# Row-maxima instructions on VectorE: own 8-bit pieces for the throw-away output in place of one shared bf16 tile

## The chip, the cores and the metric

The kernel runs on one core of a Trainium2 chip. The metric is the device time of one execution in microseconds. The kernel before took 447.98 us in the median of three runs (447.98 to 450.43). The profiled execution is one more run of the same program, with its own span.

## What is computed

An attention layer with a cumulative bias feeds a soft mixture of experts. Cut to what matters here:

```python
def _attn_ref(q, k, v, s):            # 8 batches, 8 heads, 576 positions, head size 64
    scores = scale * np.matmul(q, k.transpose(0, 1, 3, 2))
    cum = np.cumsum(np.maximum(s, 0.0), axis=-1)
    bias = -(cum[:, :, :, None] - cum[:, :, None, :])
    scores = np.where(causal, -1000000000.0, scores + np.minimum(bias, 0.0))
    scores = scores - np.max(scores, axis=-1, keepdims=True)
    attn = np.exp(scores)
    attn = attn / (np.sum(attn, axis=-1, keepdims=True) + 1e-09)
    return np.matmul(attn, v)
```

The result, as 4608 rows of 512, goes through a soft routing to 8 experts with 4 slots each (two softmaxes of x @ phi, one over rows and one over slots), two matrix products per expert, and a product back to 4608 x 512 outputs. The part of interest is `np.max(scores, axis=-1)`, the maximum of each row of scores.

## The kernel before, in words

**Stages.** The first stage, up to about 352 us, is attention. Its unit is a pair p of heads (32 pairs, four to a batch, the two heads on partitions 0 to 63 and 64 to 127 of the operands). Weights of the experts are fetched beside it as far as there is room. Then follow the end of the last batch, the experts (L960, L994) and the product back to the outputs (L1026 to L1030).

**One pair.** ScalarE splits the loaded q and k into a rounded part (L282, `cast`) and VectorE into the rest (L287, `low`). TensorE makes the scores once in a rough form for the maxima alone (L315, `mxp`, tile `mx`): queries on partitions, keys along the columns, in four groups i, each into two PSUM banks, one for each head a. VectorE takes the row maxima from these banks (L327, `red`). POOL splits the maxima into two parts (L342, L343, `f0`, tile `mh`), TensorE turns them (L350), ScalarE copies them, and a small DMA lays them into a tile `g` beside the cumulative sums (L363, `md`). Then TensorE makes the exact scores, transposed and with maxima and bias already subtracted (L381, `sc`, tile `s`), ScalarE exponentiates (L392), POOL cuts the causal triangle (L399) and adds up columns for the row sums (L425 to L431), TensorE multiplies with v (L482, tile `y`) and adds up the sums (L511, tile `sum`).

**Once a batch.** VectorE inverts the sums (L599, L600), they make a round trip through HBM (L604, then L521, tile `rs`), VectorE scales each pair's result (L544, `nr`), TensorE transposes it (L552) and works out the logits (L623, L627), and the routing's softmaxes follow (L668 to L783).

**PSUM.** The tiles `mx`, `s` and some others share six banks. A group of `mx` or of `s` takes two. A bank of `mx` is free again when VectorE has read it, a bank of `s` when ScalarE has.

**The row maxima.** One call of `red` handles one group for one head. A pair has 12 such instructions: two of 288 columns with the mask (group 0, chunk 4 of the queries), two each of 320 and 192 columns (group 3), two each of 448 and 64 columns (group 2; the one of 64 columns lies on partitions 64 to 127), and two of 288 columns that start from group 0's maxima (group 1, the scalar `m[:, a, 4:5]`). Each adds the mask to the scores, takes the maximum along the columns and writes that to a column of the tile `mx0`, `mx1` or `mx2` in SBUF. On the chip it is two instructions: the main one (`CUSTOM_DVE_ANT_0`), which also writes every sum of score and mask to a tile called `junk` that nobody reads, and a short one (`DVE_READ_ACCUMULATOR2_ANT`) that writes out the maximum. `junk` is one bf16 tile of 128 x 448 with a single buffer, so each main instruction writes over what the one ahead of it wrote.

**Order.** Every engine runs its instructions in the order that the function `schedule` sets at build time from a table of priorities (`PR`) and estimated durations. The framework then adds semaphore waits where two instructions touch the same bytes and at least one writes. An engine's own semaphore counts its finished instructions; VectorE's is called `DVE_49`. An instruction carries one wait; a second one stands ahead of it as an `EVENT_SEMAPHORE` of its own.

Of the kernel before, what the change touches and what calls it, by code (L numbers as in the profile page):

```python
# [11 lines left out]
BF16 = mybir.dt.bfloat16  # L12
# [90 lines left out]
def tile_attn_softmoe(ctx: ExitStack, tc, qk, v, s, phi, w1, w2, cst, out):  # L103
# [42 lines left out]
    ar, o = {}, 0  # L146
# [16 lines left out]
    one = actx.enter_context(tc.tile_pool(name="one", bufs=1))  # L163
    p2 = actx.enter_context(tc.tile_pool(name="p2", bufs=2))
# [37 lines left out]
    cumd = pd.tile([NH, 2, S], F32, tag="cum", name="cumd", bufs=1)  # L202

    ph = one.tile([128, HP, NS], F32, name="ph")


    mask = one.tile([128, S], F32, name="mask")
# [42 lines left out]
    def own(kind, i, n):  # L250
        live[kind, i % n] = i
# [4 lines left out]
    def scores(p):  # L256
# [4 lines left out]
        gt, w = gs[p % NG], ws[p % NW]  # L261
# [56 lines left out]
        def red(i, a):  # L318
            if i == 0 and a == 0:
                own("mx", p, 3)  # L320
            ps = st["m", p, i][a]
            for (d, c, lo, hi) in groups[i]:
                r = slice(64, 128) if c == 0 else slice(0, 128)
                w = hi - lo
                o = 576 - sum(QC[c]) + lo
                junk = p2.tile([128, 448], BF16, tag="junk", name="junk", bufs=1)
                nc.vector.tensor_tensor_reduce(  # L327
                    out=junk[r, 0:w], in0=ps[r, d:d + w], in1=mask[r, o:o + w], scale=1.0,
                    scalar=m[:, a, 4:5] if i == 1 else NEG, op0=ALU.add, op1=ALU.max, accum_out=m[r, a, c:c + 1])
        mxt = (265, 265, 560, 490)  # L330
        rdt = (480, 540, 900, 760)
        for i in range(4):
            op(("mx", p, i), "PE", mxt[i], (tu, ("mx", i)), (mxp, i),
               [("cast", p, 0), ("cast", p, 1), ("cum", p), dep("f0", old(3))], bank=2, mode=1)
            for a in range(2):
                op(("red", p, i, a), "DVE", rdt[i], (tu + 0.1 * a, ("red", i)), (red, i, a),
                   [("mx", p, i), ("red", p, 0, a) if i else None], frees=[(("mx", p, i), a)])
# [539 lines left out]
    for i in range(o // F):  # L877
        d = []
# [63 lines left out]
    def bk(name):  # L942
        return ps4.tile([128, 512], F32, tag="bk", name=name)

    ps = bk("sit")
# [173 lines left out]
```

## Time and profile before

| | |
|---|---|
| median of three runs | 447.98 us (447.98 to 450.43) |
| profiled execution, from first to last instruction | 447.8 us |
| granted TensorE clock, mean | 0.980 |
| TensorE busy | 414.7 us, 93% |
| VectorE busy | 317.0 us, 71% |
| POOL busy | 279.7 us, 62% |
| ScalarE busy | 250.8 us, 56% |
| main instructions of the row maxima | 384 (320 without and 64 with the scalar) |

In the rows below a line begins with the place in the code, the engine and the operation, then the tile written and the tiles read. PE is TensorE, DVE is VectorE, ACT is ScalarE, SP is the queue that issues DMAs. A busy TensorE is not TensorE at its peak, since the ends of matmuls are modelled and a slow sequence reads as busy too. The chain is the one that ended last, followed back from the last instruction to whatever released it.

### The profile page before, as it was taken

Reading aid. Unit: us, or ns where it says so; the run is one execution under the profiler, and the core shown is the slowest. Engines: PE = TensorE matmul, PEld = TensorE weight load, DVE = VectorE, ACT = ScalarE, POOL = GpSimd, SP = SyncE. Lnnn points to the kernel's source line nnn. Section 1 sums busy time; section 2 is a strip of 40 time slices with the busy share of each in tenths; the row PEclk is TensorE's granted clock in tenths of the full one; section 3 lists DMA queues with packets and bytes.
Section 4 is the critical chain, followed back from the end, with each engine's and each line's share of the span. In section 5 each row is a group of like instructions: output and inputs, shape, how many; then the busy total and the mean of one; then the engine's idle time right before and its main releaser. Section 6 shows DMA issues by size and latency. Waiting matters only on the chain.

```text
span 447.8 us, 14714 instructions
## 1 busy us (share of the span) xinstructions
PE 414.7 (93%) x5637; PEld 310.4 (69%) x5637; DVE 317.0 (71%) x1038; ACT 250.8 (56%) x732; POOL 279.7 (62%) x384
## 2 busy tenths in 40 slices
PE   8889999899999998999899989999999998898960
PEld 8767777687677777877677767778777776434550
DVE  7787778767888787688887887788878575221460
ACT  3146776476558664867486648666755765121350
POOL 8049888758796986588769876987888720000000
PEclk9999999899999998999999999999999999999995
DMA  5416456545554565356455643363337489999988
GB/s 173 146 46 202 152 156 206 139 127 166 167 161 145 177 186 144 113 178 186 124 146 180 182 133 101 118 162 92 103 88 200 132 271 356 344 389 410 347 276 293
DMA packets 54549, 83.01 MB, mean 185 GB/s; under 512 B 5456, under 2 KB 41936, under 8 KB 54480
## 3 DMA queue, kind: packets, MB, share of 16 engines
q1 hardware_dynamic: 54480, 82.09, 58.4%
q8 instruction: 44, 0.72, 0.7%
q14 instruction: 25, 0.20, 0.2%
HBM read 71.64 MB, written 10.06 MB: 182 GB/s over the span
## 4 chain that ended last, share of the span: by engine, by line
PE 67%; DVE 13%; DMA 5%; issue 5%; POOL 4%; ACT 2%; SPq 1%; DVEq 0%; POOLq 0%
PE s L381 20%; PE y L482 13%; DVE junk L327 9%; PE mx L315 9%; PE sum L511 4%; PE m L994 3%; PE m L960 3%; DMA arena<-rs 3%; PE busy L920 3%; DMA rs<-sr 2%; PE nat L552 2%; PE po L1026 2%; DVE arena L544 2%; PE lt L623 1%; PE mt L350 1%
## 5 line engine op out<-in xcount | busy, mean ns | idle before, releaser
L327 DVE CUSTOM_DVE_ANT_0 junk<-mx,mask 128x448 bf16<-128x448 f32 (+2 forms) x320 | 138.0, 431 | 48.5 <-PE mx L315 18.9
L392 ACT ACTIVATE arena<-s 128x288 f32<-128x288 f32 (+4 forms) x384 | 119.0, 397 | 39.0 <-PE s L381 37.9
L381 PE MATMUL s<-w 64*128 64x288 f32 (+4 forms) x1152 | 116.6, 308 | 7.0 <-DVE mx L327 6.4
L381 PEld LDWEIGHTS s<-w 64*128 64x128 f32 (+1 forms) x1152 | 88.4, 179 | 18.4 <-DVE mx L327 6.2
L482 PE MATMUL y<-arena 128*64 128x512 f32 (+4 forms) x640 | 93.1, 428 | 1.3 <-ACT arena L494 0.9
L399 POOL TENSOR_SCALAR_AFFINE_SELECT arena<-arena 128x256 f32<-128x256 f32 (+1 forms) x160 | 69.5, 452 | 22.7 <-ACT arena L392 22.3
L482 PEld LDWEIGHTS y<-arena 128*64 128x64 f32 x640 | 41.1, 136 | 46.5 <-issue 31.4
L425 POOL TENSOR_TENSOR arena<-arena 128x896 f32<-128x896 f32 x31 | 68.1, 2197 | 2.8 <-PE sum L511 0.5
L381 PE MATMUL s<-g 64*128 64x288 f32 (+4 forms) x384 | 66.3, 294 | 0.0
L315 PE MATMUL mx<-w 64*128 64x288 f32 (+4 forms) x384 | 61.1, 304 | 2.3 <-DVE acc L783 1.1
L315 PE MATMUL mx<-g,ones 64*128 64x288 f32 (+4 forms) x384 | 56.9, 302 | 0.0
L287 DVE TENSOR_TENSOR w<-arena,w 128x576 fp32r<-128x576 f32 x64 | 49.9, 813 | 1.4 <-ACT w L282 1.4
L342 POOL TENSOR_SCALAR mh<-mx 128x10 fp32r<-128x10 f32 x32 | 20.9, 654 | 46.3 <-DVE mx L327 46.2
L427 POOL TENSOR_TENSOR arena<-arena 128x640 f32<-128x640 f32 x31 | 48.0, 1550 | 2.6
L282 ACT CAST w<-arena 128x576 fp32r<-128x576 f32 x64 | 39.8, 678 | 12.1 <-DMA arena<-in_qk_dram 12.1
L315 PEld LDWEIGHTS mx<-w 64*128 64x128 f32 x384 | 41.7, 187 | 4.8 <-DVE mx L327 1.7
L381 PEld LDWEIGHTS s<-g 64*128 64x128 f32 (+1 forms) x384 | 44.3, 180 | 0.1
L315 PEld LDWEIGHTS mx<-g,ones 64*128 64x128 f32 x384 | 41.4, 187 | 0.6
L327 DVE CUSTOM_DVE_ANT_0 junk<-mx,mask,mx 128x288 bf16<-128x288 f32 x64 | 33.2, 518 | 9.3
L544 DVE TENSOR_TENSOR arena<-arena 128x576 f32<-128x576 f32 x31 | 31.1, 1031 | 3.9 <-DMA arena<-rs 3.8
L429 POOL TENSOR_TENSOR arena<-arena 128x384 f32<-128x384 f32 x31 | 31.5, 1015 | 2.4
L559 ACT COPY arena<-nat 128x512 f32<-128x512 f32 x32 | 17.5, 588 | 25.8 <-PE nat L552 24.8
(158 smaller groups left out, 548.7 us busy)
## 6 DMA issues: line engine op xcount, KB each, us to landing
pre<-in_w_dram SPq DMA_DIRECT2D x38, 512.0 KB
arena<-in_qk_dram SPq DMA_DIRECT2D x32, 576.0 KB
arena<-in_w_dram SPq DMA_DIRECT2D x19, 512.0 KB
arena<-rs SPq DMA_DIRECT2D x62, 144.0 KB
arena<-in_v_dram SPq DMA_DIRECT2D x32, 256.0 KB
out_dram<-arena SPq DMA_DIRECT2D x11, 512.0 KB
out_dram<-pre SPq DMA_DIRECT2D x6, 512.0 KB
wg<-in_w_dram SPq DMA_DIRECT2D x5, 512.0 KB
```

The costliest lines, as they stand in the source:

```text
L282: nc.scalar.copy(w[:, QO + S * i:QO + S * (i + 1)], st["raw", p][:, i, :])
L287: nc.vector.tensor_tensor(w[:, QO + S * (2 + i):QO + S * (3 + i)], st["raw", p][:, i, :], w[:, QO + S * i:QO + S * (i + 1)].bitcast(F32), ...
L315: nc.tensor.matmul(ps[a][:, d:d + hi - lo], l[r], t[r, KO + lo:KO + hi], start=t is w, stop=t is gt)
L327: nc.vector.tensor_tensor_reduce(out=junk[r, 0:w], in0=ps[r, d:d + w], in1=mask[r, o:o + w], scale=1.0, scalar=m[:, a, 4:5] if i == 1 else ...
L381: nc.tensor.matmul(ps[a][0:n, d:d + hi - lo], t[r, ko + 128 * j:ko + 128 * j + n], t[r, qo + lo:qo + hi], start=x == 0, stop=x == 3)
L392: nc.scalar.activation(st["p", p][0:n, a, o + lo:o + hi], ps[0:n, d:d + hi - lo], AF.Exp, bias=0.0, scale=0.125)
L399: nc.gpsimd.affine_select(d, d, pattern=[[0, 2], [1, n]], compare_op=ALU.is_ge, fill=0.0, base=0, channel_multiplier=-1)
L425: eng.tensor_tensor(z[:, :, 128:576], pt[:, :, 128:576], pt[:, :, 576:1024], op=ALU.add)
L427: eng.tensor_tensor(z[:, :, 256:576], z[:, :, 256:576], pt[:, :, 1024:1344], op=ALU.add)
L429: eng.tensor_tensor(z[:, :, 384:576], z[:, :, 384:576], pt[:, :, 1344:1536], op=ALU.add)
L482: nc.tensor.matmul(y[r, lo - 64:512], vt[:, j, r], st["p", p][:, g, OFF[j] + lo - 128 * j:OFF[j] + 576 - 128 * j], start=(j == 0), stop=(j ...
L544: nc.vector.tensor_tensor(u, u, st.pop(("r", p)), op=ALU.mult)
```

## The change

The shared tile `junk` goes. One tile of 128 x 2 x 1600 bytes is made at the start in the pool `one`, and each main instruction writes into its own piece of it, as 8-bit unsigned numbers: one half for each head a, and in it 64, 192, 320 and 448 bytes for the chunks c = 0, 1, 2, 3 and twice 288 bytes for chunk 4 (groups 1 and 0).

```diff
     ph = one.tile([128, HP, NS], F32, name="ph")
+    junk = one.tile([128, 2, 1600], mybir.dt.uint8, name="junk")
...
                 o = 576 - sum(QC[c]) + lo
-                junk = p2.tile([128, 448], BF16, tag="junk", name="junk", bufs=1)
+                k = [0, 64, 256, 576, 1024][c] + (288 if i == 0 else 0)
                 nc.vector.tensor_tensor_reduce(
-                    out=junk[r, 0:w], in0=ps[r, d:d + w], in1=mask[r, o:o + w], scale=1.0,
+                    out=junk[r, a, k:k + w], in0=ps[r, d:d + w], in1=mask[r, o:o + w], scale=1.0,
                     scalar=m[:, a, 4:5] if i == 1 else NEG, op0=ALU.add, op1=ALU.max, accum_out=m[r, a, c:c + 1])
```

The number and order of instructions on every engine stay as they were; a line is added, so that L327 becomes L328. What changes is waits. In the two places below, `ISA junk` is a main instruction and `ISA mx_108` or `mx_110` a short one (the rows left out are short ones alike).

On VectorE, group 3 of pair 10 stood thus before (it opens the run that begins at 202.21 us in the trace; the last row is the `low` that follows that run, which waits for ScalarE and for a DMA, but not for VectorE):

```order
L327 ISA junk,mx_108<-mx_10_0_2053,mask 128x320 [waits PE_49]
L327 ISA mx_108 128x1
L327 ISA junk,mx_108<-mx_10_0_2053,mask 128x192 [waits DVE_49]
...
L327 ISA junk,mx_108<-mx_10_1_2054,mask 128x320 [waits DVE_49,PE_49]
...
L327 ISA junk,mx_108<-mx_10_1_2054,mask 128x192 [waits DVE_49]
...
L287 TENSOR_TENSOR w_134<-arena,w_134 128x576 [waits DMAHW5_49,Activation_49]
```

and stands thus with the change:

```order
L328 ISA junk,mx_108<-mx_10_0_1932,mask 128x320 [waits PE_49]
L328 ISA mx_108 128x1
L328 ISA junk,mx_108<-mx_10_0_1932,mask 128x192
...
L328 ISA junk,mx_108<-mx_10_1_1933,mask 128x320 [waits PE_49]
...
L328 ISA junk,mx_108<-mx_10_1_1933,mask 128x192
...
L288 TENSOR_TENSOR w_135<-arena,w_135 128x576 [waits DMAHW5_49,Activation_49]
```

Every wait of VectorE on itself is gone here, and with it the second wait.

The same group of pair 11, a little later on VectorE (from 213.76 us), is another case. Before:

```order
L327 ISA junk,mx_110<-mx_11_0_2245,mask 128x320 [waits DVE_49,PE_49]
L327 ISA mx_110 128x1
L327 ISA junk,mx_110<-mx_11_0_2245,mask 128x192 [waits DVE_49]
...
L327 ISA junk,mx_110<-mx_11_1_2246,mask 128x320 [waits DVE_49,PE_49]
```

With the change:

```order
L328 ISA junk,mx_110<-mx_11_0_2112,mask 128x320 [waits DVE_49,PE_49]
L328 ISA mx_110 128x1
L328 ISA junk,mx_110<-mx_11_0_2112,mask 128x192 [waits DVE_49]
...
L328 ISA junk,mx_110<-mx_11_1_2113,mask 128x320 [waits DVE_49,PE_49]
```

Here waits of the same name stay, but they are for another instruction: no longer the short one just ahead, but the one that last wrote the same piece, which is the same group of the pair before. Over the whole program 364 of the 384 main instructions waited for VectorE itself before, and 118 do with the change.

## The prediction

> **What bounds the kernel now.** I read the page first, its chain above all, then the chain cut into blocks, then the waits, then VectorE's instructions one by one.
>
> ```profile
> PE 414.7 (93%) x5637; PEld 310.4 (69%) x5637; DVE 317.0 (71%) x1038; ACT 250.8 (56%) x732; POOL 279.7 (62%) x384
> ...
> PE 67%; DVE 13%; DMA 5%; issue 5%; POOL 4%; ACT 2%; SPq 1%; DVEq 0%; POOLq 0%
> PE s L381 20%; PE y L482 13%; DVE junk L327 9%; PE mx L315 9%; PE sum L511 4%; PE m L994 3%; PE m L960 3%; DMA arena<-rs 3%; PE busy L920 3%; DMA rs<-sr 2%; PE nat L552 2%; PE po L1026 2%; DVE arena L544 2%; PE lt L623 1%; PE mt L350 1%
> ```
>
> TensorE is busy nearly throughout and holds two thirds of the chain. VectorE holds an eighth, and most of that is the one line that the change touches: 9% of 447.8 us, some 40 us. An average says nothing of where, so I cut the chain of the attention stage into blocks (us from the span's start; the windows are, in the rows' order, 12 to 38, 66 to 92, 101 to 136, 155 to 181, 200 to 226, 245 to 270, and for comparison 289 to 312).
>
> ```profile
> by line: DVE junk L327 39.2%; PE s L381 8.6%; issue 8.3%; POOL arena L425 8.0%; PE mx L315 6.7%; ACT arena L392 6.3%; POOL arena L427 6.0%; POOL arena L429 5.5%; POOL arena L431 3.3%; PE busy L920 2.5%; DVE mx L327 2.1%; POOL arena L399 1.6
> by line: DVE junk L327 17.2%; DMA arena<-rs 14.5%; PE s L381 14.3%; issue 13.5%; DMA rs<-sr 10.8%; SPq L521 7.4%; PE sum L511 4.0%; PE mx L315 4.0%; PE lt L623 3.4%; PE nat L552 3.4%; PE lt L627 1.7%; PE nat L635 1.7%; PE mt L350 1.6%; DVE
> by line: PE s L381 16.8%; DVE junk L327 14.1%; PE y L482 11.3%; POOL arena L425 7.1%; POOL arena L399 6.9%; issue 5.8%; PE mx L315 5.6%; PE nat L552 5.4%; DVE en L706 3.8%; ACT arena L392 2.7%; PE lt L623 2.5%; POOL mh L342 2.0%; DVE acc L7
> by line: DVE junk L327 34.3%; PE s L381 15.9%; DVE arena L544 12.6%; issue 8.9%; PE mx L315 3.9%; PE nat L552 3.4%; PE lt L623 3.4%; POOL mh L342 2.9%; PE sum L511 2.5%; DVE mx L327 2.4%; POOL mh L343 2.1%; PE lt L627 1.7%; PE nat L635 1.7%
> by line: DVE junk L327 32.9%; PE s L381 12.8%; issue 12.3%; DVE arena L544 10.7%; PE lt L623 3.4%; PE nat L552 3.4%; PE sl L775 3.3%; PE mx L315 3.1%; POOL mh L342 2.7%; DVE mx L327 2.5%; PE sum L511 2.5%; POOL mh L343 2.1%; PE lt L627 1.7%
> by line: DMA arena<-rs 21.3%; DVE junk L327 16.2%; issue 14.8%; PE s L381 12.7%; SPq L521 7.6%; PE mx L315 6.7%; PE lt L623 3.5%; PE nat L552 3.5%; PE sum L511 2.5%; PE lt L627 1.8%; PE nat L635 1.7%; PE mt L350 1.7%; PE x L471 1.5%; SPq L8
> by line: PE s L381 34.9%; PE y L482 23.8%; PE mx L315 14.6%; PE nat L552 8.3%; PE sum L511 5.5%; PE lt L623 3.8%; PE mt L350 2.7%; PE x L471 2.2%; PE lt L627 1.9%; PE nat L635 1.9%; PE ln L661 0.5%; PE ln L660 0.5%
> ```
>
> The first six blocks are the start and the places where one batch ends and the next begins. There the row maxima hold 14% to 39% of the chain: 10.2, 4.5, 4.9, 8.9, 8.6 and 4.1 us (share times length), 41.2 us in all, so nearly all of the line's 40 us on the page. In the last block, and in what lies between the blocks, they hold nothing: TensorE sets the pace, and a faster VectorE is worth nothing there. After 348 us no row maxima run.
>
> The waits say how VectorE holds the others up.
>
> ```profile
> PE s L381 <- DVE mx L327: 6.4, 11, 0.8
> POOL mh L342 <- DVE mx L327: 46.2, 29, 7.1
> ACT w L282 <- DMA arena<-in_qk_dram: 12.1, 3, 6.3
> ```
>
> TensorE waits for maxima because the banks of `mx` come free only when VectorE has read them; POOL waits 29 times for a pair's last maximum.
>
> **The change part by part.** No instruction is added or removed. What goes is the wait of a main instruction for the short one ahead of it. Its price stands in VectorE's timeline (start, duration, both us):
>
> ```profile
> 200.01 0.08 DVE L327 DVE_READ_ACCUMULATOR2_ANT mx<- 128x1 f32 x1
> 200.01 0.23 DVE L599 TENSOR_SCALAR sr<-sum 128x72 f32<-128x72 f32 x1
> ...
> 202.21 0.49 DVE L327 CUSTOM_DVE_ANT_0 junk<-mx,mask 128x320 bf16<-128x320 f32 x1 [0.70 <-PE mx L315]
> 202.63 0.08 DVE L327 DVE_READ_ACCUMULATOR2_ANT mx<- 128x1 f32 x1
> 202.75 0.36 DVE L327 CUSTOM_DVE_ANT_0 junk<-mx,mask 128x192 bf16<-128x192 f32 x1
> 203.03 0.08 DVE L327 DVE_READ_ACCUMULATOR2_ANT mx<- 128x1 f32 x1
> 203.26 0.49 DVE L327 CUSTOM_DVE_ANT_0 junk<-mx,mask 128x320 bf16<-128x320 f32 x1
> ...
> 204.85 0.08 DVE L327 DVE_READ_ACCUMULATOR2_ANT mx<- 128x1 f32 x1
> 204.97 0.23 DVE L327 CUSTOM_DVE_ANT_0 junk<-mx,mask 64x64 bf16<-64x64 f32 x1
> 205.13 0.08 DVE L327 DVE_READ_ACCUMULATOR2_ANT mx<- 64x1 f32 x1
> 205.35 0.62 DVE L327 CUSTOM_DVE_ANT_0 junk<-mx,mask 128x448 bf16<-128x448 f32 x1
> ...
> 207.07 0.52 DVE L327 CUSTOM_DVE_ANT_0 junk<-mx,mask,mx 128x288 bf16<-128x288 f32 x1
> 207.51 0.08 DVE L327 DVE_READ_ACCUMULATOR2_ANT mx<- 128x1 f32 x1
> 207.51 1.42 DVE L287 TENSOR_TENSOR w<-arena,w 128x576 fp32r<-128x576 f32 x2
> ```
>
> This is a run of ten main instructions (320, 192, 320, 192, 448, 64, 448, 64, 288, 288 columns) of pair 10. From the start of a short instruction to the start of the next main one it takes 0.12 us (202.63 to 202.75) where the main one waits for VectorE alone, and 0.23 us (203.03 to 203.26) where it waits for TensorE as well and so has a wait instruction ahead of it. The run has four steps of the first kind and five of the second: 4 x 0.12 + 5 x 0.23 = 1.63 us out of the 5.30 us between 202.21 and 207.51.
>
> How much of it goes? Two rows show a short instruction followed by something that does not wait for VectorE: L599 starts at the same 200.01, L287 at the same 207.51. And L287 has waits of its own (for ScalarE and a DMA) which were met by then and cost nothing. So the step falls to about 0, and a run takes 1.63 us less. That is the upper end. The lower end: the main instruction, being of the same kind, may have to let the short one finish; then 0.08 us stay in each of nine steps, and the run gains 0.9 us. Between them lies the instruction of 64 columns, which starts at partition 64 while its neighbours start at 0: if it and the one behind it let everything ahead finish, four steps keep 0.08 us, and the run gains 1.3 us. The Trainium skill has that as a rule ("VectorE: DVE Perf Modes", section "Two Vector instructions with no wait between them"): an instruction whose operands start in another quarter of the partitions than those before starts only when all earlier ones have finished. No row of before shows this rule at work, since every such instruction waits anyway; by it the run would gain the 1.3 us.
>
> The same pages speak against the change as a whole. The Trainium skill ("VectorE: DVE Perf Modes", sections "The DRAIN you can't avoid" and "Rules for kernel authors") says that VectorE empties its pipeline after every instruction, and that chained instructions gain nothing by leaving semaphores out; by that the sum below would be 0. The rows of L599 and L287 above speak against it.
>
> 118 main instructions keep a wait for VectorE, for the instruction that wrote the same piece a pair earlier. That one is a dozen instructions back, so the wait is met; it costs nothing by the row of L287, and up to the 0.23 - 0.12 = 0.11 us of a separate wait instruction if that can't run ahead.
>
> The 8-bit output itself: no row shows an 8-bit write. The nearest ones:
>
> ```profile
> L327 DVE CUSTOM_DVE_ANT_0 junk<-mx,mask 128x448 bf16<-128x448 f32 x64 | 40.0, 625 | 9.6 <-PE mx L315 0.8
> L327 DVE CUSTOM_DVE_ANT_0 junk<-mx,mask 64x64 bf16<-64x64 f32 x64 | 14.6, 227 | 2.2
> L544 DVE TENSOR_TENSOR arena<-arena x31: 747/764/2668, 75.5 to 371.6; 128x576 f32<-128x576 f32 x31
> ```
>
> From 64 to 448 columns the duration grows by 398 ns, 1.04 ns a column, on top of 161 ns. L544 writes 576 columns of four bytes, and its median (the middle of the three numbers) is 764 ns; the line of the two-byte outputs gives 161 + 576 x 1.04 = 760. Two bytes or four cost the same, so I take one byte at the same price. A gain is excluded, as the pace is one column whatever the width. The dear end would be a slower pace: a run has 2624 columns, so 0.6 ns more a column would eat the 1.63 us.
>
> **The sum.** Ten main instructions of a run are busy for 2 x (0.49 + 0.36 + 0.62 + 0.23 + 0.52) = 4.4 us, and 1.63 us goes with them: 0.37 us for each us of busy time on the chain. The blocks then give 3.8, 1.7, 1.8, 3.3, 3.2 and 1.5 us. Two of them are cut short. At the start ScalarE's split of pair 1 waits up to 6.3 us for its load (the third of the waits above), and what VectorE gains on pair 0 ahead of it, one run, is lost there: 3.8 - 1.6 = 2.2. The other cut is TensorE's own pace, seen from when pairs' exact scores begin:
>
> ```profile
> 155.25 0.78 PE s L381 x7
> 181.44 0.77 PE s L381 x6
> 200.90 0.78 PE s L381 x7
> 225.57 0.78 PE s L381 x7
> 289.15 0.78 PE s L381 x7
> 311.43 0.78 PE s L381 x7
> ```
>
> The last block, with TensorE alone on the chain, takes 22.3 us; the one at 155 takes 26.2, the one at 200 takes 24.7, for two pairs and a batch's end each. So the block at 200 can give no more than 2.4, where the sum says 3.2. That makes 2.2 + 1.7 + 1.8 + 3.3 + 2.4 + 1.5 = 12.9 us. With 1.3 us a run it is 10.7, with 0.9 us 7.5 (cut in the same way). What is late next is POOL:
>
> ```profile
> 207.69 0.69 POOL L342 TENSOR_SCALAR mh<-mx 128x10 fp32r<-128x10 f32 x1 [1.44 <-DVE mx L327]
> 210.33 3.50 DVE L544 TENSOR_TENSOR arena<-arena 128x576 f32<-128x576 f32 x2
> 210.73 2.49 POOL L425 TENSOR_TENSOR arena<-arena 128x896 f32<-128x896 f32 x1
> ```
>
> POOL waits only 1.44 us for the end of that run, so a gain of 1.63 would be cut to 1.44 where POOL's maxima are on the path. And a second L544 that meets POOL's L425 ends when that one does: 3.50 us for the two instead of 1.5. L425 comes earlier too, as it stands behind the maxima, so I let that stall move along. I take 11.5 us, between 10.7 and 12.9. All of it lies before 348 us, and what follows (the last batch, the fetching of weights into room that attention leaves, the experts) begins when attention ends, so it shifts as a whole. 447.8 - 11.5 = 436.3 us for a profiled execution; the median stands 0.2 us above the profiled one, so 436.5 us.
>
> **The rivals.** First, the short instruction holds the next main one, so only 0.9 us a run go, and POOL and TensorE's pace cut some of it: a gain of 4.5 to 7.5 us, 440.5 to 443.5, in the middle 442. For it: nothing in the trace shows two pairs of main and short instruction without a wait. Against it: L599 and L287.
>
> Second, no gain that counts: the gap after an instruction is time that VectorE needs anyway, and the wait merely fills it, or POOL, which is busy 62% overall and adjoins every run, closes the path at once. (The first is what the Trainium skill's rule on the emptied pipeline, named above, would make of the change.) The time is then 448, within 1% (about what a measurement of this kernel can tell from no change). Against it: a start at 200.01 beside the short instruction at 200.01, and L599's 0.23 us there, which is just 161 ns plus 72 columns, so it wasn't stretched.
>
> Third, slower: VectorE reaches L287 and L544 at other times and meets POOL's additions more often. The row of L544 prices it: 2668 ns at worst against 764, so 1.9 us a meeting, on the path in the blocks. What all of them cost at L544 now comes from its mean on the page:
>
> ```profile
> L544 DVE TENSOR_TENSOR arena<-arena 128x576 f32<-128x576 f32 x31 | 31.1, 1031 | 3.9 <-DMA arena<-rs 3.8
> ```
>
> That is 31 x (1031 - 764) ns = 8.3 us. It decides from the seventh new meeting on (7 x 1.9 = 13.3 us, over the gain); ten would give 447.98 - 11.5 + 19 = 455.5. Against it: L425 and the maxima move together, and there are only six blocks to meet in.
>
> Fourth, the change doesn't do what it says: if the 118 waits that stay were to hold as those before did, about a third of the gain would be lost, to 440. The order of the pieces speaks against it.
>
> **How the numbers follow.** Forecast, a gain of 9 to 14 us: 0.56. More than 14, if the stalls at L425 shrink too: 0.05. First and fourth rival, 4.5 to 9 us: 0.19. Second: 0.14. Third, or a dear 8-bit write: 0.06. So faster by over 1% 0.80, within 1% 0.14, slower 0.06. The time is that of the forecast. Low end: all 15.3 us of the uncut sum and one stall less, 430.8, say 431. High end: a gain of 3 us, 445, which leaves out most of the second rival and the third.
>
> **What would show it.** Right: in runs such as that at 202 us the main instructions follow each other with the next start at the start of the short one; the mean duration of each form stays (625 ns for 448 columns); the row maxima's share of the chain falls in the blocks, and the blocks at 155 and 200 come near 22 us; L381 waits less than 6.4 us for maxima. Wrong: steps of 0.08 us or more behind each short instruction (first rival), durations that grow (the 8-bit write), gone steps but blocks as long as before with POOL or L544 on the chain (second and third).

## The result and the profile after

The changed kernel takes 434.59 us in the median of four runs (432.45 to 436.21), the kernel before beside it 447.98 us (446.13 to 450.43). The ratio is 0.968, with a 95% interval of 0.963 to 0.973. The profiled execution has a span of 433.4 us against 447.8. The prediction said 436.5 us, in a range of 431 to 445.

One thing ahead has to be put right. The text on the change and the prediction call the runs at 202.21 and 213.76 us those of pairs 10 and 11. Counted through the trace they are those of pairs 18 and 19; pair 10's run begins at 114.22 us, pair 11's at 123.97. In the trace pair 18 has the waits that are shown there for pair 10 (none left on VectorE), pair 19 those shown for pair 11 (a wait on an older instruction left), so no number changes.

First the run of pair 18 again, in VectorE's timeline with the change (start, duration, both us):

```profile
189.69 0.49 DVE L328 CUSTOM_DVE_ANT_0 junk<-mx,mask 128x320 uint8<-128x320 f32 x1 [0.71 <-PE mx L316]
190.10 0.08 DVE L328 DVE_READ_ACCUMULATOR2_ANT mx<- 128x1 f32 x1
190.10 0.35 DVE L328 CUSTOM_DVE_ANT_0 junk<-mx,mask 128x192 uint8<-128x192 f32 x1
...
191.61 0.08 DVE L328 DVE_READ_ACCUMULATOR2_ANT mx<- 128x1 f32 x1
191.73 0.23 DVE L328 CUSTOM_DVE_ANT_0 junk<-mx,mask 64x64 uint8<-64x64 f32 x1
191.88 0.08 DVE L328 DVE_READ_ACCUMULATOR2_ANT mx<- 64x1 f32 x1
192.00 0.62 DVE L328 CUSTOM_DVE_ANT_0 junk<-mx,mask 128x448 uint8<-128x448 f32 x1
...
193.81 0.08 DVE L328 DVE_READ_ACCUMULATOR2_ANT mx<- 128x1 f32 x1
```

From 189.69 to the last short instruction at 193.81 are 4.12 us, where the run took 5.30. The next main instruction starts with the short one (190.10 and 190.10), except around the one of 64 columns: 0.12 us ahead of it (191.61 to 191.73) and 0.12 us behind it (191.88 to 192.00) are still there.

A pair that keeps a wait on an older instruction, pair 19:

```profile
201.49 0.08 DVE L328 DVE_READ_ACCUMULATOR2_ANT mx<- 128x1 f32 x1
201.49 0.35 DVE L328 CUSTOM_DVE_ANT_0 junk<-mx,mask 128x192 uint8<-128x192 f32 x1
```

It steps as fast (201.49 and 201.49): a wait that is met costs nothing.

The durations by form, from the groups of lines (busy us, mean ns):

```profile
L328 DVE CUSTOM_DVE_ANT_0 junk<-mx,mask 128x448 uint8<-128x448 f32 x64 | 39.8, 622 | 2.0 <-PE mx L316 1.0
L328 DVE CUSTOM_DVE_ANT_0 junk<-mx,mask 64x64 uint8<-64x64 f32 x64 | 14.6, 228 | 1.6
```

622 and 228 ns against 625 and 227: the 8-bit write neither gains nor costs.

The chain of the page, and the chain of two blocks, the start (12 to 34 us) and the batch end at 146 to 169:

```profile
PE s L382 20%; PE y L483 13%; PE mx L316 9%; DMA arena<-rs 5%; PE m L995 4%; PE sum L512 4%; PE m L961 3%; DMA rs<-sr 3%; PE nat L553 2%; SPq L522 2%; DVE junk L328 2%; DMA arena<-in_qk_dram 2%; PE po L1027 2%; PE lt L624 2%; PE sl L776 1%
```

```profile
by line: DMA arena<-in_qk_dram 20.3%; ACT arena L393 12.4%; PE busy L921 9.9%; POOL arena L426 9.5%; POOL arena L428 9.0%; PE s L382 8.3%; PE mx L316 7.7%; POOL arena L430 6.4%; ACT w L283 5.7%; issue 2.0%; POOL arena L432 2.0%; DVE junk L3
by line: DMA arena<-rs 19.1%; issue 16.4%; PE s L382 16.3%; SPq L522 12.0%; DVE junk L328 8.4%; PE mx L316 8.2%; PE lt L624 3.8%; PE nat L553 3.8%; PE sum L512 2.8%; PE lt L628 1.9%; PE nat L636 1.9%; SPq L841 1.6%; DVE mx L328 1.4%; PE mt 
```

The row maxima fell from 9% of the chain to 2%. At the start the load of a pair and POOL's additions took their place, at the batch end the round trip of the inverted sums through HBM (`DMA arena<-rs`, its issue `SPq L522`): 31% of the block at 146 us. The row of the same block before, at 155 us, does not name it as far as it is printed.

The prediction also named the length of two blocks as a sign: 26.2 and 24.7 us before, near 22 if it was right. With the change the same two blocks go from one of these starts of exact scores to the next:

```profile
145.87 0.78 PE s L382 x7
169.39 0.78 PE s L382 x8
188.37 0.78 PE s L382 x7
211.72 0.78 PE s L382 x7
```

That is 23.5 and 23.4 us, so this sign came only in part.

The waits for maxima:

```profile
PE s L382 <- DVE mx L328: 2.2, 4, 0.6
POOL mh L343 <- DVE mx L328: 17.3, 18, 5.3
DVE junk L328 <- PE mx L316: 42.8, 46, 1.8
```

TensorE waits 2.2 us for them instead of 6.4, POOL 17.3 instead of 46.2, and VectorE now waits 42.8 us for TensorE, where line L327 waited 18.9.

Where the time came from, from the start of each pair's transpose (L350, then L351) in the two traces, in us:

| stretch | before | after | change |
|---|---|---|---|
| start, to pair 2's transpose | 38.05 | 33.76 | -4.3 |
| five batch ends (pairs 7; 9 to 11; 15; 19; 23) | 89.8 | 82.6 | -7.2 |
| the other 22 pairs | 223.5 | 218.0 | -5.5 |
| after the last pair's transpose | 96.4 | 99.0 | +2.6 |

Together that is 14.4 us, the difference of the two spans. But not all of it is the change, for the granted TensorE clock was not the same in the same places. The page gives it in 40 slices of the span, in tenths of full speed; the first row is of before, the second of the change. The third row is a stretch of before, with its granted clock as the third number from the end:

```profile
PEclk9999999899999998999999999999999999999995
PEclk9999999999999999999999999999999998999996
174.00:176.00 2.00, 2.00 (x19) 2.00 (x17) 2.00 (x4) 1.05 (x5) 1.57 (x3) 0.50 0.01 2
```

The execution of before had half the clock for two spells of 3.4 us, from 85.2 and from 173.9 us, and both lie in batch ends: those of pairs 7 and 15 took 15.06 and 15.04 us, those of pairs 19 and 23, with the whole clock, 13.51 each. In `shared_u8` below, which keeps every wait, no spell fell there, all four took 13.5 us, and the row of the batch ends reads 86.7. So about 3.1 of the 7.2 us are the clock of one execution. The change is worth 4.1 us at the batch ends by these two profiles, and 4.5 and 5.3 by two further ones of the changed kernel, in which the row reads 82.2 and 81.4: no more than the 5.5 us between the ends.

In the execution of the change a spell of 3.4 us lies behind the last pair instead, from 356.5 us. That is a part of the last row, but not all. Two further executions of the changed kernel, below, took 98.9 us there with one spell and 101.9 with three times its length; `own_bf16` and `two_buf`, with none, took 98.5 and 97.5; the two kernels that keep every wait, with none either, 96.4 and 96.6. So 1 to 2 us of that row may well belong to the change, and what causes them is open, as is what sets the spells.

### The profile page after: what moved, and what is told of

It is laid out like the page before. It is cut to its first block, busy times and chain, and to the rows that moved or that the text cites. A ratio compares the mean times of both kernels' runs of the same rounds, so it can differ in the third digit from the quotient of the medians.

```text
span 433.4 us, 14579 instructions
## 1 busy us (share of the span) xinstructions
PE 404.0 (93%) x5637; PEld 303.1 (70%) x5637; DVE 305.6 (71%) x1038; ACT 249.0 (57%) x732; POOL 280.3 (65%) x384
## 4 chain that ended last, share of the span: by engine, by line
PE 67%; DMA 10%; DVE 5%; issue 4%; POOL 4%; SPq 3%; ACT 3%; DVEq 0%; POOLq 0%
PE s L382 20%; PE y L483 13%; PE mx L316 9%; DMA arena<-rs 5%; PE m L995 4%; PE sum L512 4%; PE m L961 3%; DMA rs<-sr 3%; PE nat L553 2%; SPq L522 2%; DVE junk L328 2%; DMA arena<-in_qk_dram 2%; PE po L1027 2%; PE lt L624 2%; PE sl L776 1%
## 5 line engine op out<-in xcount | busy, mean ns | idle before, releaser
L328 DVE CUSTOM_DVE_ANT_0 junk<-mx,mask 128x448 uint8<-128x448 f32 (+2 forms) x320 | 125.1, 428 | 46.3 <-PE mx L316 42.8
L393 ACT ACTIVATE arena<-s 128x288 f32<-128x288 f32 (+4 forms) x384 | 118.8, 399 | 26.8 <-PE s L382 24.7
L382 PE MATMUL s<-w 64*128 64x288 f32 (+4 forms) x1152 | 107.5, 302 | 2.2 <-DVE mx L328 2.2
L382 PEld LDWEIGHTS s<-w 64*128 64x128 f32 (+1 forms) x1152 | 81.4, 177 | 9.8 <-PE nat L553 2.5
L316 PE MATMUL mx<-w 64*128 64x288 f32 (+4 forms) x384 | 56.8, 302 | 1.6 <-DVE acc L784 1.1
L382 PE MATMUL s<-g 64*128 64x288 f32 (+4 forms) x384 | 58.1, 290 | 0.0
L288 DVE TENSOR_TENSOR w<-arena,w 128x576 fp32r<-128x576 f32 x64 | 52.9, 859 | 1.7 <-ACT w L283 1.7
L316 PE MATMUL mx<-g,ones 64*128 64x288 f32 (+4 forms) x384 | 53.4, 301 | 0.0
L316 PEld LDWEIGHTS mx<-w 64*128 64x128 f32 x384 | 38.0, 185 | 3.8 <-DVE acc L784 1.4
L316 PEld LDWEIGHTS mx<-g,ones 64*128 64x128 f32 x384 | 38.1, 185 | 1.2 <-DMA g<-cumd 0.2
L545 DVE TENSOR_TENSOR arena<-arena 128x576 f32<-128x576 f32 x31 | 31.4, 1022 | 8.2 <-DMA arena<-rs 8.0
L382 PEld LDWEIGHTS s<-g 64*128 64x128 f32 (+1 forms) x384 | 36.4, 177 | 0.4
L343 POOL TENSOR_SCALAR mh<-mx 128x10 fp32r<-128x10 f32 x32 | 20.4, 638 | 17.3 <-DVE mx L328 17.3
L328 DVE DVE_READ_ACCUMULATOR2_ANT mx<- 128x1 f32 (+1 forms) x384 | 31.3, 82 | 0.0
```

Of the source, the lines that this page charges most:

```text
L288: nc.vector.tensor_tensor(w[:, QO + S * (2 + i):QO + S * (3 + i)], st["raw", p][:, i, :], w[:, QO + S * i:QO + S * (i + 1)].bitcast(F32), ...
L316: nc.tensor.matmul(ps[a][:, d:d + hi - lo], l[r], t[r, KO + lo:KO + hi], start=t is w, stop=t is gt)
L328: nc.vector.tensor_tensor_reduce(out=junk[r, a, k:k + w], in0=ps[r, d:d + w], in1=mask[r, o:o + w], scale=1.0, scalar=m[:, a, 4:5] if i == ...
L382: nc.tensor.matmul(ps[a][0:n, d:d + hi - lo], t[r, ko + 128 * j:ko + 128 * j + n], t[r, qo + lo:qo + hi], start=x == 0, stop=x == 3)
L393: nc.scalar.activation(st["p", p][0:n, a, o + lo:o + hi], ps[0:n, d:d + hi - lo], AF.Exp, bias=0.0, scale=0.125)
L545: nc.vector.tensor_tensor(u, u, st.pop(("r", p)), op=ALU.mult)
```

## The experiments

**Is it the wait or the type?** The change does two things at once. Two kernels do one alone.

`own_bf16`, pieces without the 8-bit type:

```diff
-    junk = one.tile([128, 2, 1600], mybir.dt.uint8, name="junk")
+    junk = one.tile([128, 1600], BF16, name="junk")
...
-                k = [0, 64, 256, 576, 1024][c] + (288 if i == 0 else 0)
+                k = [0, 64, 256, 576, 1024][c] + (288 * a if c == 4 else 0)
...
-                    out=junk[r, a, k:k + w], in0=ps[r, d:d + w], in1=mask[r, o:o + w], scale=1.0,
+                    out=junk[r, k:k + w], in0=ps[r, d:d + w], in1=mask[r, o:o + w], scale=1.0,
```

> Bf16 as before, but pieces: one row of 1600 bf16 columns, where instructions that follow each other never share a piece (the two heads share the pieces of the chunks 0 to 3). What is left out against the change is the 8-bit type alone. Theory of the waits (the gain comes from a main instruction no longer waiting for the short one just ahead): the next main instruction of a run starts with the short one, runs of ten near 4.1 us, time as with the change, 433 to 437 us, though more instructions keep a wait that is already met. Rival, the 8-bit write itself is cheaper (fewer bytes into SBUF): time as before, 446 to 450. Between the two if a met wait costs: 130 waits on the short instruction two back at 0.1 us each, of which a quarter on the chain, 437 to 440.

Measured: 434.27 us, ratio 0.963 (0.957 to 0.968). The steps are those of the change, the bf16 pieces notwithstanding.

`shared_u8`, the 8-bit type without the pieces:

```diff
-                junk = p2.tile([128, 448], BF16, tag="junk", name="junk", bufs=1)
+                junk = p2.tile([128, 448], mybir.dt.uint8, tag="junk", name="junk", bufs=1)
```

> One shared tile as before, but of 8-bit numbers: the type changed alone. Theory of the waits: every main instruction waits as before, steps of 0.12 and 0.23 us between a short and the next main instruction, main durations as before (625 ns for 448 columns), 446 to 450 us. Rival, the 8-bit write is what gains: 433 to 440. Rival of the prediction, the 8-bit write is dear: durations grow, over 450.

Measured: 448.74 us, ratio 0.998 (0.994 to 1.003), so no difference. Its timeline has the steps of before, 0.12 us (200.02 to 200.14) and 0.23 us (200.42 to 200.65):

```profile
200.02 0.08 DVE L327 DVE_READ_ACCUMULATOR2_ANT mx<- 128x1 f32 x1
200.14 0.36 DVE L327 CUSTOM_DVE_ANT_0 junk<-mx,mask 128x192 uint8<-128x192 f32 x1
200.42 0.08 DVE L327 DVE_READ_ACCUMULATOR2_ANT mx<- 128x1 f32 x1
200.65 0.49 DVE L327 CUSTOM_DVE_ANT_0 junk<-mx,mask 128x320 uint8<-128x320 f32 x1
```

The two together settle it: the whole effect is the wait, and the type only makes the pieces small.

**How far back must the wait reach?** `two_buf` gives the bf16 tile of before a second buffer, nothing else:

```diff
-                junk = p2.tile([128, 448], BF16, tag="junk", name="junk", bufs=1)
+                junk = p2.tile([128, 448], BF16, tag="junk", name="junk", bufs=2)
```

> The tile of before, bf16, with two buffers in turn in place of one: each main instruction then waits for the short instruction two back instead of the one just ahead. Theory that only the wait on the instruction just ahead costs and a met wait is free: 433 to 437 us, the next main instruction starts with the short one. If a met wait costs its own wait instruction (0.1 us each where there are two waits): runs of ten lose some 0.5 us against the change, 438 to 442. Rule that leaving waits out gains nothing: 446 to 450.

Measured: 432.45 us, ratio 0.958 (0.951 to 0.964), by one digit of the code. 344 of the 384 main instructions still wait for VectorE here, with a separate wait instruction wherever there are two waits, but for a short instruction two back or more, and that one is done:

```profile
189.53 0.49 DVE L327 CUSTOM_DVE_ANT_0 junk<-mx,mask 128x320 bf16<-128x320 f32 x1 [0.70 <-PE mx L315]
189.94 0.08 DVE L327 DVE_READ_ACCUMULATOR2_ANT mx<- 128x1 f32 x1
189.94 0.35 DVE L327 CUSTOM_DVE_ANT_0 junk<-mx,mask 128x192 bf16<-128x192 f32 x1
```

A second group of runs asked whether it is better than the change.

> The bf16 tile of before with two buffers in turn, once more, beside the change itself on one chip. Theory that the wait on the instruction just ahead is all that counts: same time as the change within 0.5%. Rival, it is the faster of the two, as its first ratio to before (0.958 against 0.963 to 0.968) hints: 1 to 4 us under the change.

Measured: 434.09 us, ratio 0.963 (0.959 to 0.967). The change in the same group:

> The change itself, beside the other two on the same chip: ratio to before 0.960 to 0.970.

Measured: 436.82 us, ratio 0.967 (0.962 to 0.972). The intervals overlap; the two can't be told apart.

**What holds the 64-column instruction?** `full64` runs it on all partitions:

```diff
-                r = slice(64, 128) if c == 0 else slice(0, 128)
+                r = slice(0, 128)
```

> The change, with the instruction of 64 columns run on all 128 partitions instead of partitions 64 to 127; the lower half holds no queries of the pair, and what it writes there nobody reads. In the profile of the change the steps ahead of and behind that instruction stayed at 0.11 us while the others fell to 0. Theory that the start partition holds them: all nine steps of a run fall to 0, runs of ten go from 4.1 to about 3.7 us, and by the same share as in the sum 2 to 4 us are gained against the change, 430.5 to 433. Rival, it is the short length (the short instruction and its write end later than the next could start): steps stay at 0.11 us, 433 to 437. Rival, steps fall but other work sets the pace by now: 433 to 436 with runs of 3.7 us.

Measured: 435.12 us, ratio 0.962 (0.956 to 0.968). The steps are gone:

```profile
190.38 0.08 DVE L328 DVE_READ_ACCUMULATOR2_ANT mx<- 128x1 f32 x1
190.38 0.22 DVE L328 CUSTOM_DVE_ANT_0 junk<-mx,mask 128x64 uint8<-128x64 f32 x1
190.53 0.08 DVE L328 DVE_READ_ACCUMULATOR2_ANT mx<- 128x1 f32 x1
190.53 0.62 DVE L328 CUSTOM_DVE_ANT_0 junk<-mx,mask 128x448 uint8<-128x448 f32 x1
```

The length is still 64 columns, so it is not the short length that held the step. Two things changed together, the start partition and the number of partitions. The number alone doesn't hold: at the end of attention, in the profile of the change, an addition on partitions 0 to 63 (L432) stands between two instructions on 128 partitions, and it starts, as the next main instructions do, 0.08 us before the one ahead ends:

```profile
348.86 0.32 DVE L703 CAST en<-e_nat 128x160 fp32r<-128x160 f32 x1 [0.22 <-PE cta L714]
349.10 0.28 DVE L432 TENSOR_TENSOR arena<-arena 64x128 f32<-64x128 f32 x1
```

That leaves the start partition. The Trainium skill ("VectorE: DVE Perf Modes", section "Two Vector instructions with no wait between them") says just that: an instruction that starts in another quarter of the partitions than the one before starts when all earlier ones have finished. The trace agrees, 0.12 us against 0. But the time is that of the change: in the profile attention ends 0.5 to 1.1 us earlier (the last pair's transpose at 333.3 us, in three executions of the change at 333.8 to 334.4), and the runs don't show it. VectorE mostly waits for TensorE by now; and its `low` (L288) takes 996 ns in the mean here, as against 859 in the change, since 36 of the 64 run beside one of POOL's additions and 24 there. How much of that lay on the path is not shown.

**Where is a faster VectorE worth something?** The table above says: at the start and the batch ends, but also between them, where the prediction saw nothing to gain. Two kernels give own pieces to one half of the pairs and one shared 8-bit tile to the other:

```diff
+    shared = one.tile([128, 448], mybir.dt.uint8, name="shared")
...
-                    out=junk[r, a, k:k + w], in0=ps[r, d:d + w], in1=mask[r, o:o + w], scale=1.0,
+                    out=junk[r, a, k:k + w] if p in (0, 1, 2, 6, 7, 9, 10, 14, 15, 18, 19, 22, 23) else shared[r, 0:w], in0=ps[r, d:d + w], in1=mask[r, o:o + w], scale=1.0,
```

(`others_only` has `p not in`.) The change itself ran beside them.

> The change itself once more, beside the kernels of this group, so that they are compared on one chip. Ratio to before 0.963 to 0.973.

> Own pieces only for the pairs whose maxima lie in the start and at the batch ends (pairs 0, 1, 2, 6, 7, 9, 10, 14, 15, 18, 19, 22, 23); the other pairs share one tile, of 8-bit numbers, as before. As the prediction had it (a faster VectorE is worth nothing between the blocks): the whole gain, ratio 0.963 to 0.973. Theory from the profile of the change, in which the stretches between the blocks became shorter too, by 4.0 us in all: a ratio of 0.973 to 0.981, that is 3 to 5 us less gain than the change.

> The other half: own pieces only for the pairs that lie between the blocks, the 13 pairs of the blocks share one 8-bit tile. As the prediction had it: no gain, ratio 0.998 to 1.002. Theory from the profile of the change: 3 to 5 us gained, ratio 0.989 to 0.994, with a pair between the blocks taking 8.9 us from one start of exact scores to the next as against 9.2 before.

Measured: the change 434.04 us, ratio 0.964 (0.959 to 0.968); `blocks_only` 437.61 us, 0.973 (0.967 to 0.979); `others_only` 446.67 us, 0.992 (0.988 to 0.996). The 27 thousandths of the blocks and the 8 of the rest make 35 of the whole's 36, with 6 and 4 thousandths of doubt either way. The 8 are under one percent, but clear of none, which is what the prediction had. What a pair between the blocks takes is seen from two neighbouring starts of exact scores on the chain, here of `blocks_only` (with the shared tile there) and of `others_only` (with own pieces there):

```profile
34.37 0.78 PE s L383 x8
43.60 0.78 PE s L383 x6
```

```profile
55.76 0.78 PE s L383 x6
64.67 0.78 PE s L383 x6
```

9.23 us with the shared tile, 8.91 us with own pieces. Why, when TensorE was busy throughout? TensorE's timeline shows it, before and after, for the same part of a pair:

```profile
62.66 0.88 PE L381 MATMUL s<-w 64*128 64x288 f32 x6
63.25 0.41 PE L381 MATMUL s<-g 64*128 64x288 f32 x2
...
64.64 0.42 PE L315 MATMUL mx<-w 64*128 64x288 f32 x2
...
65.12 0.71 PE L511 MATMUL sum<-arena,onesl 128*32 128x72 f32 x32
```

```profile
57.71 0.56 PE L382 MATMUL s<-w 64*128 64x288 f32 x6
58.10 0.29 PE L382 MATMUL s<-g 64*128 64x288 f32 x2
...
59.49 0.29 PE L316 MATMUL mx<-w 64*128 64x288 f32 x2
...
59.85 0.71 PE L512 MATMUL sum<-arena,onesl 128*32 128x72 f32 x32
```

The six matmuls `s<-w` take 0.59 us to the next row before (62.66 to 63.25) and 0.39 us after (57.71 to 58.10); from `mx` to `sum` it is 0.48 and 0.36 us. The two differences make 0.32 of the 0.33 us. The rows of TensorE's matmuls name no wait; a matmul that stands in the queue reads as busy, 0.88 us long for what takes 0.56. The rows of its weight loads (PEld) name it, here one of the timeline and one of the waits, both of before:

```profile
62.88 0.43 PEld L381 LDWEIGHTS s<-w 64*128 64x128 f32 x5 [0.17 <-DVE mx L327]
PEld s L381 <- DVE mx L327: 6.2, 24, 0.9
```

So the matmul of one head needs a bank that VectorE reads late in the pair's run, and waits for that. The other head's has gone ahead, and from there on the two heads, which with the change start together, run 0.13 us apart: the two matmuls `mx<-w` take 0.42 us from the first start to the last end, and 0.29 after, which is the second difference. With the change the waits have no such row of L382.

**What became of the end?** The last batch's inverted sums go through HBM as those of the others do. The first half of that trip, the write, took 8.25 us on the chain before (from 358.84) and 9.12 us in the profile of the change:

```profile
341.82 9.12 DMA rs<-sr
```

`late_get` holds the weight fetches back until it is issued:

```diff
-        op(("get", i), "SP", 460, (200.0 + i,), (get, a), d + ([last] if a[0] == "w" else []), dma=1456)
+        op(("get", i), "SP", 460, (200.0 + i,), (get, a), d + ([last] if a[0] == "w" else []) + [("rd", NP - 2)], dma=1456)
```

> The change, with the fetches of weights into room that attention leaves held back until the last round trip of inverted sums is issued. Theory that this round trip, 8.3 us before and 9.1 us with the change as against 2.8 us for the same trip early in the kernel, waits behind those fetches in the DMA queues: the trip falls to about 3 us and the scaling of the last batch begins 4 to 7 us earlier; whether the time falls depends on the weights, which come later by as much: 428 to 437 us. Rival, the trip is long for another reason: it stays above 7 us, and the time is that of the change or longer.

Measured: 433.30 us, ratio 0.962 (0.957 to 0.967), against 0.964 for the change in the same group. In SP's timeline the read, which waits for the write, is issued 2.2 us after it (341.24 to 343.41), the weights from 344.70 on:

```profile
341.24 0.33 SPq L605 DMA_DIRECT2D rs<-sr  x1
343.41 1.25 SPq L522 DMA_DIRECT2D arena<-rs  x2
344.70 0.58 SPq L841 DMA_DIRECT2D arena<-in_w_dram  x1
```

So the write does wait behind the fetches, and 7 us of it can be had back, but the runs show nothing won. The fetches that start at 311.30 us in the profile of the change beside it start at 344.70 here, and after the last transpose the kernel takes 98.1 us, as against 98.9 there. That stretch held 6.8 us of half clock here and 3.4 there, so a gain of a us or two may hide behind the clock; no run separates that.

Both later steps together:

> The change with both later steps: the 64-column instruction on all 128 partitions and the weight fetches held back until the last round trip of inverted sums is issued. In the profiles the first made attention 1.1 us shorter (the last pair's transpose at 333.3 instead of 334.4 us), the second the rest 0.8 us shorter (98.1 instead of 98.9). If both add up: 2 us under the change, a ratio between the two of 0.995 to 0.997, which five rounds may just not tell from none. Rival, the rest of the kernel gives it back, as it varied by more than that between the profiles (96.4 to 102.0 us): no difference from the change.

Measured: 431.96 us, ratio 0.960 (0.955 to 0.964), beside the change's 0.967 (0.962 to 0.972). The last pair's transpose comes at 333.0 us instead of 333.8, what follows takes 98.0 us instead of 101.9 (`both` had 6.8 us of half clock behind the last pair, the change 10.2). The intervals overlap by a little, so whether it beats the change stays open; it beats the kernel before, as all but `shared_u8` do (`others_only` by 0.8% alone).

## Why the prediction was right, point by point

**The bound.** Right for the blocks in kind: the row maxima were what the chain waited for there, and most of them have left it (8.4% of the block at 146 us, where they held 34.3% before). Wrong between the blocks, in the step "a faster VectorE is worth nothing there". It rested on TensorE being busy and alone on the chain, and a stalled matmul counts as busy. It was worth some 0.33 us in 14 of these 22 pairs and 5.5 us in all by the table; `others_only` measured 0.4% to 1.2%, 2.0 to 5.6 us.

**The step.** The price of the waits, 0.12 and 0.23 us, was right, and their fall to 0 too, read from the two rows in which something without a wait followed a short instruction. The middle case held: four of nine steps stay, not at the 0.08 us that I gave them but at 0.12, so a run gains 1.18 us instead of 1.3. Met waits and the 8-bit write cost nothing, as taken. The rule by which leaving semaphores out gains nothing (second rival) is refuted for these instructions by `two_buf`, 0.958.

**The sum.** Start and batch ends were to give 12.9 us, and I took 11.5. The two profiles differ there by 11.5, but 3.1 of it are the two spells of half clock before, so that the agreement is luck: with the whole clock they gave 4.3 + 4.1 = 8.4 us. (`blocks_only` alone, whose pairs reach a little into the stretches between, was 2.1% to 3.3% faster, 9 to 15 us, which can't tell these sums apart.) The start gave 4.3 us instead of 2.2: the first run's gain was indeed lost at the load of pair 1 (its split began at 16.63 us before and 16.77 after), but what follows gained more than its steps. I take it that VectorE and TensorE waited for each other's banks in turn there, so that a step saved was saved twice; no run here separates that. The batch ends gave 4.1 instead of 10.7 (5.3 at most, in the further execution above): the runs gained less, and the round trip of the sums, not POOL, was late next, as the block's row above shows. I had cut only one block by TensorE's pace, and none by this trip; and the 26.2 us of the block at 155, against 24.7 for the one at 200, held one of the spells of half clock, which I had not looked for.

**The rest.** "It shifts as a whole" held for the order of things, but in the two profiles 2.6 us came back after the last pair. A part is the spell of half clock there; 1 to 2 us are not, and the forecast had put this at nothing.

**The rivals.** That a short instruction holds the next one holds only where the start partition changes. That VectorE meets POOL's additions more often came true in a small way: 24 of the 64 instructions of the first line below run beside one for over 0.3 us, where 3 did before, and those 24 take 1026 ns in the mean. The two lines in the groups of the changed kernel:

```profile
L288 DVE TENSOR_TENSOR w<-arena,w 128x576 fp32r<-128x576 f32 x64 | 52.9, 859 | 1.7 <-ACT w L283 1.7
L545 DVE TENSOR_TENSOR arena<-arena 128x576 f32<-128x576 f32 x31 | 31.4, 1022 | 8.2 <-DMA arena<-rs 8.0
```

The mean of the first went from 813 to 859 ns, 64 x 46 ns = 2.9 us, that of the second from 1031 to 1022; far from the seven meetings that would have eaten the gain. The waits that stay are met.

So the median of 434.6 us lies 1.9 under the forecast, but not because each term held. The mechanism was right and the step was priced right. The batch ends gave 6.6 us less than was added up for them, the stretch between them 5.5 us that was put at nothing, and the start 2 us more; that these cancel so closely is luck.

## What to carry to other kernels

An output that nobody reads still orders the instructions that write it: with one buffer each waits for the one ahead to have finished, and a second buffer takes that away as well as a piece for each does. Read the price of such a wait from the row in which something without it follows the same instruction. And where an engine is busy throughout, look at what its weight loads wait for, and compare the length of the same few instructions in two places, before calling a wait worth nothing: stalled matmuls read as busy. And before two profiles are subtracted stretch by stretch, look at the granted clock in both.

## What the runs showed of the hardware

A main instruction behind a short one starts 0.12 us later when its first partition is 64 and the one before started at 0, with no wait between them at all; where both start at 0 it starts at once. A semaphore wait for an instruction two back, met by then, takes no time, even as a wait instruction of its own ahead of the main one. Bf16 and 8-bit outputs take the same time, 622 ns for 448 columns in the change and in `own_bf16`. A small write to HBM, 2.2 us with the fetches held back (`late_get`), took 9.1 us when it was issued behind fetches of 512 KB. And a spell of half clock of 3.4 us, in a stretch that TensorE fills, made a batch end 1.5 us longer (15.05 against 13.51 us).
